# Nine weight and cache buffers as one tile, and some loads made into one load each, in a decode step with sliding-window attention and a gated unit

## The chip, the cores and the metric

The kernel runs on one core of one Trainium2 chip. A core has TensorE (PE, matrix products; PEld is its loading of the stationary operand), VectorE (DVE), ScalarE (ACT), GpSimd (POOL) and SyncE (SP), and 16 DMA engines that move data between the chip's memory (HBM) and the on-chip memory (SBUF). Matrix products land in a second on-chip memory, PSUM. The metric is the device time of one execution in microseconds (us); before the change its median is 199.18 us over three runs, which lie between 199.14 and 199.29.

## The reference

One token for each of B = 8 sequences, D = 512 wide. `s` is attention with 32 query heads over 8 shared key/value heads, on the last W = 2048 of 8192 cached positions; `g` is a gated unit 1792 wide. All inputs are bfloat16.

```python
xn = layernorm(x)
q = (xn @ wq).reshape(B, 1, 32, 128)             # wq 512 x 4096
k, v = k_cache[:, :, -W:], v_cache[:, :, -W:]    # 8 heads of 128, each for 4 query heads
s = (softmax(q k^T * 128**-0.5) v).reshape(B, 1, 4096) @ wo   # wo 4096 x 512
g = (sigmoid(xn @ w_gate) * (xn @ w_up)) @ w_down             # 512 x 1792, 512 x 1792, 1792 x 512
out = x + s * silu(g)
```

Keys and values of the window are 32 MB (2^20 bytes) each, wq and wo 4 MB each, the three other weights 1.75 MB each: some 81 million bytes are read, each once.

## The kernel before

**What is loaded.** SBUF holds nine buffers, `slot0` to `slot8`, of up to 16 KB on each of 128 partitions. Every large load takes one buffer: a tile of keys or values (half of a sequence's heads, 2 MB, `want_cache`, line 156), the gate and the up weights (`want_rows`, line 96, each in two loads of two rows per partition), the first 1408 rows of the down weights (`want_down`), and the remaining 384 rows of the down weights in eight small loads into one buffer called `side` (`want_side`, 5, 9, 5, 9, 3, 9, 3 and 9 partitions). The query weights take two buffers (rows 0 and 1, rows 2 and 3), with three side loads behind each. The output weights take four buffers: 16, 10, 4 and 2 of the 32 rows that each partition holds.

**What orders the loads.** The list `todo` holds all of them in the order of lines 171 to 192: gate, up, down, two side loads, first half of the query weights, three side loads, second half, three side loads; then key tiles with the value tiles three places behind; then the output weights. `pump` takes from the list's head as long as a buffer is empty, and `free` gives a buffer back and pumps again. So each load stands in SP's instruction queue in that order, and waits there for the last reader of the buffer's earlier content. Each load also signals its landing on one of eight completion semaphores, which all loads take in turn, those that ACT issues too: a load waits until the load eight places before it has landed. The input `x` is loaded by ACT (line 195).

**What is computed, in order of PE's queue.** Layer norm of x (DVE, ACT), its transpose, the gate product (line 278), the up product (line 294), 26 small transposes (line 328), the query product (line 352: four rows of wq, eight matmuls each; the first 16 matmuls need the first load of wq, the last 16 the second), the down product (line 366), the transposes that spread the queries, and the unit's last steps. Then the attention: for each sequence 16 half units, in each of which `k_transposes` makes eight transposes of a key tile (line 456) that DVE copies (line 461), and every second of which brings `scores` (line 474). `row_max` (line 487 and the exponentials of line 494), `p_transposes` (line 563) and `values` (line 584) follow one to three sequences behind. Lines 672 to 701 finish the last three sequences; the final tile of values is used in lines 697 and 698, and the last `turn` (line 701) writes the last column of `oP_sb`.

**The end.** The output product (lines 703 to 714) needs all of `oP_sb`. For each of the 32 rows `t` of wo it makes four matmuls (128x32 by 128x128), side by side in four column groups of the array:

```python
for t in range(RT):
    for j in range(NB):
        nc.tensor.matmul(fin_ps[Z * j : Z * (j + 1), :], lhsT=oP_sb[:, t, :],
                         rhs=weights[("wo_sb", t)][:, j * P : (j + 1) * P], ...)
```

Its first matmul waits for the load of rows 0 to 15, and those of rows 16, 26 and 30 for the three others. After it come two DVE instructions (lines 717 and 719) and four small stores.

Of the kernel before, what the change touches and what calls it, by code (L numbers as in the profile page):

```python
# [10 lines left out]
def kernel(  # L11
# [14 lines left out]
    P = 128  # L26
    B, _, D = A_x.shape
    _, Hkv, Sk, Dh = A_k_cache.shape
# [4 lines left out]
    KT = D // P  # L33
# [5 lines left out]
    CT = W // PG  # L39
# [8 lines left out]
    bf16 = mybir.dt.bfloat16  # L48
# [8 lines left out]
    slots = ctx.enter_context(tc.tile_pool(name="slots", bufs=1))  # L57
# [21 lines left out]
    q0, q1 = nc.sync, nc.scalar  # L79
    k_tiles = {}  # L80
    v_tiles = {}
    weights = {}
    rows_of = {}
    todo = []
    empty = list(range(9))

    def pump():
        while todo and (empty or not todo[0][0]):
            slot, f = todo.pop(0)
            f(f"slot{empty.pop(0)}") if slot else f()  # L90

    def free(t):
        empty.append(int(t[1][4:]))
        pump()

    def want_rows(name, w, per, r0, r1, step=None):
        def f(tag):
            t = slots.tile([P, r1 - r0, w.shape[1]], bf16, name=name, tag=tag)
            for a in range(r0, r1, step or r1 - r0):
                z = a + (step or r1 - r0)  # L100
                q0.dma_start(
                    out=t[:, a - r0 : z - r0, :],
                    in_=w.rearrange("(p r) n -> p r n", r=per)[:, a:z, :],
                )
            rows_of[(name, r0)] = (t, tag)
            for r in range(r0, r1):
                weights[(name, r)] = t[:, r - r0, :]

        todo.append((True, f))

    LOW, SF = (5, 5, 3, 3), 15
    MID, SM = 9, 4
# [3 lines left out]
    MT = 11  # L116
# [3 lines left out]
    side = {}  # L120

    def want_side(w, q, at, count, rows, base, of):
        def f(tag=None):
            if tag:
                t = slots.tile([P, SF, w.shape[1]], bf16, name="side", tag=tag)
                nc.gpsimd.memzero(t[:M_AT])  # L126
                side["t"] = t
                rows_of[("side", 0)] = (t, tag)
                for r in range(SF):
                    weights[("wd_sb", MT + r)] = t[: M_AT + MP if r < SM else SP, r]  # L130
            q0.dma_start(  # L131
                out=side["t"][at + q : at + q + 4 * (count - 1) + 1 : 4, :rows].rearrange(
                    "p s n -> p (s n)"
                ),
                in_=w[base : base + of * count * rows, :].rearrange(
                    "(p q s) n -> q p (s n)", q=of, s=rows
                )[q % of],
            )

        todo.append((not side, f))  # L140
        side["asked"] = True

    def want_down(w):
        def f(tag):
            t = slots.tile([P, MT, w.shape[1]], bf16, name="wd_sb", tag=tag)
            q0.dma_start(
                out=t[:].rearrange("p t n -> p (t n)"),
                in_=w[: MT * P, :].rearrange("(p t) n -> p (t n)", t=MT),
            )
            rows_of[("wd_sb", 0)] = (t, tag)  # L150
            for r in range(MT):
                weights[("wd_sb", r)] = t[:, r, :]

        todo.append((True, f))

    def want_cache(tiles, cache, name, b, i):
        def f(tag):
            t = slots.tile([P, CT, Dh], bf16, name=name, tag=tag)
            q0.dma_start(
                out=t[:].rearrange("p c d -> p (c d)"),  # L160
                in_=cache[b, G * i : G * (i + 1), win0:Sk, :].rearrange(
                    "l (p c) d -> p l (c d)", c=CT
                ),
            )
            tiles[(b, i)] = (t, tag)

        todo.append((True, f))

    RT = 32
    Z = 32  # L170
    want_rows("wg_sb", B_w_gate, KT, 0, KT, 2)
    want_rows("wu_sb", B_w_up, KT, 0, KT, 2)
    want_down(B_w_down)
    sides = []
    for q in range(4):
        sides.append((q, 0, LOW[q], SF, m0 + q // 2 * 2 * LOW[0] * SF, 2))
        sides.append((q, M_AT, MID, SM, m1, 4))
    for x in sides[:2]:
        want_side(B_w_down, *x)
    for i in range(2):  # L180
        want_rows("wq_sb", A_wq, KT, 2 * i, 2 * i + 2)
        for x in sides[2 + 3 * i : 5 + 3 * i]:
            want_side(B_w_down, *x)
    order = [(b, i) for b in range(B) for i in range(NQ)]
    AHEAD = 3
    for n in range(len(order) + AHEAD):
        if n < len(order):
            want_cache(k_tiles, A_k_cache, "k_sb", *order[n])
        if n >= AHEAD:
            want_cache(v_tiles, A_v_cache, "v_sb", *order[n - AHEAD])  # L190
    for t0, t1 in ((0, 16), (16, 26), (26, 30), (30, RT)):
        want_rows("wo_sb", A_wo, RT, t0, t1)

    x_bf = work.tile([B, D], bf16, name="x_bf")
    q1.dma_start(out=x_bf[:], in_=A_x.flatten_outer_dims())

    eps_t = work.tile([B, 1], f32, name="eps_t")
    nc.gpsimd.memset(eps_t[:], 1e-5)
# [8 lines left out]
        out=perm[:].rearrange("k (l p) -> k l p", l=G),  # L207
        in_=ident[:].rearrange("k (p l) -> k l p", l=G),
# [11 lines left out]
        out=rstd[:], in_=mv[:, 1:2], func=AF.Sqrt, bias=eps_t[:], scale=1.0  # L220
# [4 lines left out]
        out=xn_bf[:],  # L225
# [8 lines left out]
    for kt in range(KT):  # L234
        nc.tensor.transpose(  # L235
            out=xnT_ps[:, kt, :],
            in_=xn_bf[:].rearrange("b (p kt) -> b kt p", kt=KT)[:, kt, :],
# [53 lines left out]
    for k in range(F // FC):  # L291
        u_ps = ps_t.tile([B, FC], f32, name="u_ps", tag="t")
        for kt in range(KT):
# [8 lines left out]
            out=h_bf[:B, k * FC : (k + 1) * FC],  # L302
# [6 lines left out]
    for h in range(2):  # L309
        c = LOW[2 * h]  # L310
# [37 lines left out]
    for kt in range(KT):  # L348
        for e in range(2):
            for g in range(G):  # L350
                c0 = (G * e + g) * D
                nc.tensor.matmul(  # L352
                    q_ps[e][Z * g : Z * (g + 1), :],
                    lhsT=xnT_sb[:, kt, :],
                    rhs=weights[("wq_sb", kt)][:, c0 : c0 + D],
                    start=(kt == 0),
                    stop=(kt == KT - 1),
                    tile_position=(0, Z * g),
                    skip_group_check=True,
                )  # L360
        if kt % 2 == 1:
            free(rows_of[("wq_sb", kt - 1)])
    d_ps = ps_s.tile([P, D], f32, name="d_ps", tag="s")
    for t, k in enumerate(rows):
        g = t % G
# [206 lines left out]
    WIDE = 5  # L572

    def value(b, i, c):
        v = v_tiles[(b, i)][0][:]
        if b < WIDE:
            rows = [slice(NX * i, NX * (i + 1))]
            parts = [v.rearrange("p (j c) d -> p c j d", j=NJ)[:, c]]
        else:
            rows = [slice(Z * k, Z * (k + 1)) for k in range(NM * i, NM * (i + 1))]  # L580
            v = v.rearrange("p (m e c) d -> p m c e d", e=2, c=CU)
            parts = [v[:, m, c] for m in range(NM)]
        for r, x in zip(rows, parts):
            nc.tensor.matmul(  # L584
                o_ps[r] if b < WIDE else o_ps[r, 0:2],
                lhsT=pT[b][:, c, r],
                rhs=x,
                start=(c == 0),
                stop=(c == CU - 1),
                tile_position=(0, r.start),  # L590
                skip_group_check=True,
            )
        if c == CU - 1:
            free(v_tiles.pop((b, i)))
# [160 lines left out]
```

## Time and profile before

| | us |
|---|---|
| device time, median of three runs | 199.18 |
| device time of the profiled execution | 199.33 |
| its span, from the first to the last instruction | 197.5 |
| PE, DVE and ACT busy | 157.4, 125.4, 40.7 |
| share of the 16 DMA engines' span that the packets of SP's queue took | 96.6% |
| first matmul of the output product | 188.81 |
| first DVE instruction after the output product (line 717) | 194.19 |

The profile is one execution. Times count from the span's start. A line of its timeline reads: start, length, engine, line of the kernel, operation, out<-in, number of instructions in the group, and in brackets how long the engine was idle before it and what ended that. In the table of windows, the columns behind a stretch are its length, each engine's busy time with the number of instructions, the share of full clock that PE was granted (PEclk), the mean busy share of the 16 DMA engines, and what they moved.

### The profile page before, as it was taken

How to read it: one execution, taken by the hardware profiler on the slowest of the kernel's cores; microseconds unless marked ns; L12 is line 12 of the kernel's file. 1: busy time of each engine (PE TensorE's matmuls, PEld its weight loads, DVE VectorE, ACT ScalarE, POOL GpSimd, SP SyncE). 2: the span in 40 equal slices, each digit the busy share in tenths (PEclk: the TensorE clock that was granted, in tenths of full speed). 3: DMA queues.
4: the chain of work that ended last, by engine and by line, in shares of the span. 5: the costliest groups of instructions: out<-in, count | busy, mean ns of one | idle time of the engine just before them, and what ended most of it. 6: DMA issues, size and time to landing. Idle time of an engine off the chain costs nothing.

```text
span 197.5 us, 4796 instructions
## 1 busy us (share of the span) xinstructions
PE 157.4 (80%) x2112; PEld 103.1 (52%) x2112; DVE 125.4 (63%) x245; ACT 40.7 (21%) x95; POOL 11.0 (6%) x22
## 2 busy tenths in 40 slices
PE   0089559999788898799979987999799979976733
PEld 0034325776664565466545654566466556655531
DVE  4623106999797696679666965796669658935201
ACT  0522022006306001600160016001600160071000
POOL 8910200000000000000000000000000000000000
PEclk9999859999999999999999999999999999999975
DMA  6999999999999999999999999999999999999980
GB/s 205 424 440 435 431 434 435 425 425 431 423 425 425 438 428 435 431 425 428 422 433 431 435 425 433 428 418 428 428 438 431 428 428 431 428 423 425 428 366 21
DMA packets 6396, 81.32 MB, mean 412 GB/s; under 512 B 812, under 2 KB 820, under 8 KB 1624
## 3 DMA queue, kind: packets, MB, share of 16 engines
q1 hardware_dynamic: 6328, 81.01, 96.6%
q8 instruction: 16, 0.26, 0.5%
q10 hardware_dynamic: 48, 0.01, 0.0%
q14 instruction: 4, 0.03, 0.0%
HBM read 81.01 MB, written 0.01 MB: 410 GB/s over the span
## 4 chain that ended last, share of the span: by engine, by line
DMA 73%; PE 22%; POOL 3%; SPq 0%; issue 0%; DVE 0%; POOLq 0%
DMA v_sb<-in_A_v_cache_dram 46%; DMA wo_sb<-in_A_wo_dram 14%; PE kT_ps L456 11%; DMA wq_sb<-in_A_wq_dram 7%; DMA k_sb<-in_A_k_cache_dram 6%; PE o_ps L584 4%; PE s_ps L474 3%; POOL side L126 2%; PE m_ps L614 1%; PE fin_ps L706 1%; PE pT_ps L563 1%; SPq L131 0%; POOL perm L206 0%; POOL hT_sb L245 0%; DVE prod L717 0%
## 5 line engine op out<-in xcount | busy, mean ns | idle before, releaser
L461 DVE COPY kT_sb<-kT_ps 128x1024 bf16<-128x1024 bf16 x128 | 84.2, 683 | 28.9 <-PE kT_ps L456 25.0
L456 PE MATMUL kT_ps<-perm,k_sb 128*128 128x128 bf16 x1024 | 72.6, 220 | 3.7 <-DMA k_sb<-in_A_k_cache_dram 3.7
L456 PEld LDWEIGHTS <-k_sb 128*128 128x128 bf16 x1024 | 58.8, 98 | 26.1 <-issue 16.8
L584 PE MATMUL o_ps<-v_sb,pT_sb 128*32 128x256 bf16 (+1 forms) x352 | 36.5, 327 | 9.0 <-DMA v_sb<-in_A_v_cache_dram 7.6
L474 PE MATMUL s_ps<-kT_sb,qm_sb 128*32 128x512 bf16 x256 | 25.6, 389 | 1.3 <-DVE kT_sb L461 1.1
L494 ACT ACTIVATE p_buf<-s_ps,st 32x512 bf16<-32x512 f32 x32 | 21.7, 679 | 15.4 <-DVE st L487 15.1
L584 PEld LDWEIGHTS <-pT_sb 128*32 128x32 bf16 (+1 forms) x352 | 12.3, 101 | 21.7 <-issue 19.7
L604 ACT ACTIVATE o_sb<-o_ps,fac 128x512 f32<-128x512 f32 (+1 forms) x8 | 4.9, 608 | 60.9 <-PE o_ps L584 60.9
L568 DVE COPY pT_sb<-pT_ps 128x1024 bf16<-128x1024 bf16 x16 | 10.8, 676 | 1.8 <-PE pT_ps L563 1.8
L474 PEld LDWEIGHTS <-qm_sb 128*32 128x32 bf16 x256 | 7.0, 93 | 8.0 <-issue 1.3
L563 PE MATMUL pT_ps<-turn_rows,p_buf 128*128 128x128 bf16 x128 | 10.7, 227 | 0.0
L563 PEld LDWEIGHTS <-p_buf 128*128 128x128 bf16 x128 | 9.4, 149 | 0.2 <-issue 0.2
L521 ACT ACTIVATE w_row<-w 1x128 f32<-1x128 f32 x8 | 2.5, 309 | 30.6 <-DVE w L514 30.6
L235 PE MATMUL xnT_ps<-ident,xn_bf 8*128 8x8 bf16 x4 | 0.3, 176 | 10.6 <-DVE xn_bf L224 10.6
L385 DVE COPY qm_sb<-qT_ps 128x128 bf16<-128x128 bf16 x2 | 1.4, 881 | 8.7 <-PE qT_ps L380 8.7
L301 DVE TENSOR_TENSOR h_bf<-sig,u_ps 8x448 bf16<-8x448 f32 x4 | 2.4, 608 | 6.6 <-PE u_ps L294 6.1
L278 PE MATMUL g_ps<-wg_sb,xnT_sb 128*8 128x448 bf16 x16 | 5.7, 544 | 0.3 <-DVE xnT_sb L242 0.3
L494 ACT ACTIVATION_READ_ACCUMULATOR p_buf<-s_ps,st 32x1 f32 x32 | 5.9, 184 | 0.0
L706 PE MATMUL fin_ps<-wo_sb,oP_sb 128*32 128x128 bf16 x128 | 3.3, 263 | 3.1 <-DMA wo_sb<-in_A_wo_dram 3.1
L487 DVE TENSOR_REDUCE st<-s_ps 128x1 f32<-128x512 f32 x8 | 5.4, 681 | 0.5 <-PE s_ps L474 0.5
L235 PEld LDWEIGHTS <-xn_bf 8*128 8x128 bf16 x4 | 0.2, 117 | 10.6 <-DVE xn_bf L224 10.6
L352 PE MATMUL q_ps<-wq_sb,xnT_sb 128*32 128x512 bf16 x32 | 3.1, 526 | 3.2 <-DMA wq_sb<-in_A_wq_dram 3.2
(88 smaller groups left out, 92.0 us busy)
## 6 DMA issues: line engine op xcount, KB each, us to landing
k_sb<-in_A_k_cache_dram SPq DMA_DIRECT2D x16, 2048.0 KB
v_sb<-in_A_v_cache_dram SPq DMA_DIRECT2D x16, 2048.0 KB
wq_sb<-in_A_wq_dram SPq DMA_DIRECT2D x2, 2048.0 KB
wo_sb<-in_A_wo_dram SPq DMA_DIRECT2D x1, 2048.0 KB
wg_sb<-in_B_w_gate_dram SPq DMA_DIRECT2D x2, 896.0 KB
wu_sb<-in_B_w_up_dram SPq DMA_DIRECT2D x2, 896.0 KB
wd_sb<-in_B_w_down_dram SPq DMA_DIRECT2D x1, 1408.0 KB
wo_sb<-in_A_wo_dram SPq DMA_DIRECT2D x1, 1280.0 KB
```

The costliest lines, as they stand in the source:

```text
L126: nc.gpsimd.memzero(t[:M_AT])
L278: nc.tensor.matmul(g_ps[:], lhsT=xnT_sb[:, kt, :B], rhs=weights[("wg_sb", kt)][:, k * FC : (k + 1) * FC], start=(kt == 0), stop=(kt == KT ...
L456: nc.tensor.transpose(out=kT_ps[:, c, :], in_=k_sb[:, j * CU + h * CH + c, :], identity=perm[:],)
L461: nc.vector.tensor_copy(out=kT[(b, u)][:, h * CH : (h + 1) * CH, :], in_=kT_ps[:])
L474: nc.tensor.matmul(s_ps[b][NR * l : NR * (l + 1), :], lhsT=qm_sb[:, b, i * G + l, o : o + Z], rhs=t[:, :, PG * l : PG * (l + 1)], start=(u ...
L487: nc.vector.tensor_reduce(out=st[b][:], in_=s_ps[b][:], axis=AX.X, op=ALU.max, negate=True)
L494: nc.scalar.activation(out=p_buf[b % 2][rows, :, l, :], in_=s[rows, :].rearrange("k (c p) -> k p c", p=PG), func=AF.Exp, bias=st[b][rows, ...
L563: nc.tensor.transpose(out=pT_ps[:, c, :], in_=p_buf[b % 2][:, :, :, h * CH + c].rearrange("k p l -> k (p l)"), identity=turn_rows[:],)
L568: nc.vector.tensor_copy(out=pT[b][:, h * CH : (h + 1) * CH, :], in_=pT_ps[:])
L584: nc.tensor.matmul(o_ps[r] if b < WIDE else o_ps[r, 0:2], lhsT=pT[b][:, c, r], rhs=x, start=(c == 0), stop=(c == CU - 1), tile_position=(0 ...
L604: nc.scalar.activation(out=o[:, :n], in_=o_ps[:, :n], func=AF.Copy, scale=fac.pop(b)[:])
L706: nc.tensor.matmul(fin_ps[Z * j : Z * (j + 1), :], lhsT=oP_sb[:, t, :], rhs=weights[("wo_sb", t)][:, j * P : (j + 1) * P], start=(t == 0), ...
```

## The change

The nine buffers become one tile `ring` of [128, 9, 8192] bfloat16, and each load names a place in it (`room`). `pump` can now look for n neighbouring empty places, and holds the whole list until there are that many. `want_rows` takes a list of steps, one load each, and makes rows that lie behind each other in a partition one contiguous run.

- The up weights are one load of four rows per partition (14336 bytes on each of 128 partitions), not two of 7168. The gate weights stay two loads.
- The query weights are one load of 32768 bytes per partition over two neighbouring places, not two of 16384, and stand behind four side loads with the other four behind them.
- The output weights take two neighbouring places. Rows 0 to 25 are one load of 26624 bytes per partition, not loads of 16384 and 10240; rows 26 to 29 and 30 to 31 stay loads of their own, into the same two places.
- Both buffers of the query weights are given back together after the whole query product.
- x is loaded by four loads of two rows each. With two loads fewer for up and query weights and three more for x, the turn of the eight semaphores moves by one for the key and value tiles.

In the built program the matmuls and the other engines' instructions stand in the same order. The last half of the up product, the last half of the query product and rows 16 to 25 of the output product have no wait of their own any more: the first matmul of each product waits for the whole load. SP holds the load of the 26 rows for the last transposes of the last key tile; before, the loads of 16 and of 10 rows waited for earlier readers, and the load of 4 rows for those transposes.

```diff
-    empty = list(range(9))
+    NS = 9
+    ring = slots.tile([P, NS, CT * Dh], bf16, name="ring")
+    empty = list(range(NS))
     def pump():
-        while todo and (empty or not todo[0][0]):
-            slot, f = todo.pop(0)
-            f(f"slot{empty.pop(0)}") if slot else f()
+        while todo:
+            n, f = todo[0]
+            k = 0
+            if n:
+                found = [k for k in empty if all(k + m in empty for m in range(n))]
+                if not found:
+                    return
+                k = found[0]
+                for m in range(n):
+                    empty.remove(k + m)
+            todo.pop(0)
+            f(k)
...
+    def room(k, n, *shape):
+        size = 1
+        for x in shape:
+            size *= x
+        x = ring[:, k : k + n].rearrange("p s e -> p (s e)")[:, :size]
+        if len(shape) == 2:
+            x = x.rearrange("p (r n) -> p r n", r=shape[0])
+        return x, list(range(k, k + n))
+
+    def want_rows(name, w, per, r0, r1, steps):
+        n = -(-(r1 - r0) * w.shape[1] // (CT * Dh))
...
+            for step in steps:
                 q0.dma_start(
-                    out=t[:, a - r0 : z - r0, :],
-                    in_=w.rearrange("(p r) n -> p r n", r=per)[:, a:z, :],
+                    out=t[:, a - r0 : a - r0 + step, :].rearrange("p r n -> p (r n)"),
+                    in_=w.rearrange("(p r) n -> p r n", r=per)[
+                        :, a : a + step, :
+                    ].rearrange("p r n -> p (r n)"),
                 )
...
-    want_rows("wg_sb", B_w_gate, KT, 0, KT, 2)
-    want_rows("wu_sb", B_w_up, KT, 0, KT, 2)
+    want_rows("wg_sb", B_w_gate, KT, 0, KT, (2, 2))
+    want_rows("wu_sb", B_w_up, KT, 0, KT, (KT,))
...
-    for x in sides[:2]:
+    for x in sides[:4]:
         want_side(B_w_down, *x)
-    for i in range(2):
-        want_rows("wq_sb", A_wq, KT, 2 * i, 2 * i + 2)
-        for x in sides[2 + 3 * i : 5 + 3 * i]:
-            want_side(B_w_down, *x)
+    want_rows("wq_sb", A_wq, KT, 0, KT, (KT,))
+    for x in sides[4:]:
+        want_side(B_w_down, *x)
...
-    for t0, t1 in ((0, 16), (16, 26), (26, 30), (30, RT)):
-        want_rows("wo_sb", A_wo, RT, t0, t1)
+    want_rows("wo_sb", A_wo, RT, 0, RT, (26, 4, 2))
...
-    q1.dma_start(out=x_bf[:], in_=A_x.flatten_outer_dims())
+    for r in range(0, B, 2):
+        q1.dma_start(out=x_bf[r : r + 2], in_=A_x.flatten_outer_dims()[r : r + 2])
...
-        if kt % 2 == 1:
-            free(rows_of[("wq_sb", kt - 1)])
+    free(rows_of[("wq_sb", 0)])
```

## The prediction

> **What bounds the kernel now.** I read the page's head and slices first, then the table of windows, then the timeline around the two places that the change touches, and SP's own timeline last.
>
> ```profile
> span 197.5 us, 4796 instructions
> PEclk9999859999999999999999999999999999999975
> DMA  6999999999999999999999999999999999999980
> q1 hardware_dynamic: 6328, 81.01, 96.6%
> ```
>
> The DMA engines are busy from the first slice to the last but two. The windows say how full:
>
> ```profile
> 5.00:10.00 5.00, 0.00 (x0) 0.00 (x0) 3.19 (x5) 2.86 (x3) 5.00 (x8) 1.00 1.02 430
> 10.00:15.00 5.00, 4.17 (x15) 1.61 (x16) 1.22 (x5) 1.07 (x2) 0.44 (x2) 1.00 1.03 439
> 140.00:180.00 40.00, 35.16 (x530) 24.45 (x529) 27.60 (x57) 11.13 (x29) 0.00 (x0) 1.00 1.01 430
> 189.00:190.00 1.00, 0.89 (x64) 0.74 (x53) 0.00 (x0) 0.00 (x0) 0.00 (x0) 1.00 1.00 420
> 190.00:191.80 1.80, 0.00 (x0) 0.00 (x0) 0.00 (x0) 0.00 (x0) 0.00 (x0) 0.57 0.79 325
> 191.80:192.40 0.60, 0.54 (x24) 0.54 (x27) 0.00 (x0) 0.00 (x0) 0.00 (x0) 0.50 0.79 304
> 193.70:194.20 0.50, 0.42 (x11) 0.13 (x7) 0.01 (x1) 0.00 (x0) 0.00 (x0) 0.50 0.00 0
> ```
>
> The last column but one is the DMA share, the one before it PE's granted clock. From 5 us to 190 us the share is 1.0 at some 430 GB/s, whether the loads are of 0.9 MB (first row) or of 2 MB (third row): the stream never stops, and only a time after the stream, or a hole in it, can move the end. After 190 us the engines run out one by one, and PE's clock has fallen to half. The timeline there:
>
> ```profile
> 187.73 0.30 DVE L639 CAST oP_sb<-l_ps 128x32 bf16<-128x32 f32 x1 [0.28 <-PE l_ps L632]
> 188.81 1.08 PE L706 MATMUL fin_ps<-wo_sb,oP_sb 128*32 128x128 bf16 x64 [1.12 <-DMA wo_sb<-in_A_wo_dram]
> 191.86 2.28 PE L706 MATMUL fin_ps<-wo_sb,oP_sb 128*32 128x128 bf16 x64 [1.97 <-DMA wo_sb<-in_A_wo_dram]
> 191.86 1.06 PEld L706 LDWEIGHTS <-oP_sb 128*32 128x32 bf16 x40 [2.12 <-issue]
> 193.10 0.42 PEld L706 LDWEIGHTS <-oP_sb 128*32 128x32 bf16 x16 [0.18 <-issue]
> 193.74 0.13 PEld L706 LDWEIGHTS <-oP_sb 128*32 128x32 bf16 x7 [0.21 <-issue]
> 194.19 0.29 DVE L717 TENSOR_TENSOR prod<-gg_sb,fin_ps 128x128 f32<-128x128 f32 x1 [6.16 <-PE fin_ps L706]
> ```
>
> The output product is four bursts, one for each load of wo: 16 rows at 188.81, 10 at 191.86, 4 at 193.10, 2 at 193.74. The landings recorded for the four are 188.77, 191.82, 193.06 and 193.69, so each burst starts 0.04 us behind its load and ends before the next one lands. The time is: last landing, plus two rows, plus the finish. 64 matmuls (16 rows) took 1.08 us at full clock, 40 weight loads (10 rows) 1.06 us at half clock; read one by one, a row follows the last after 0.056 us in the first burst and after 0.107 us in the second.
>
> **The output rows, the step that sets the time.** The first 26 rows now have one landing. Loads are taken in order and the bytes ahead of row 26 are the same, so it falls where the load of 10 rows landed, 191.82, less what fewer packets save. The 16 rows that ran at 188.81 under the cover of that load have lost it: they start at 191.86 too. Before, PE waited in this stretch 0.19 us for rows 26 to 29 and 0.22 us for rows 30 and 31; those will long have landed, so 32 rows run in one piece. At half clock, with the first step 0.06 as in the burst of 191.86, the last row starts at 191.86 + 0.06 + 30 x 0.107 = 195.13, and DVE follows 0.39 us behind the last row's start, as before (193.80 to 194.19): 195.52, which is 1.33 us later. At full clock, 0.056 per row, PE would be done with row 25 by 193.3 and meet the landings of the last two loads: a cost of nothing, or a gain of about 0.1 from a faster last burst. So the ends are -0.1 and +1.33, and they are far apart.
>
> I take half clock. The nearest row is the burst at 191.86: it is the same code at the same time, and it ran at 0.50 after an idle of 1.97 us. The clock records show the fall at 190.27, 0.4 us after a burst of 1.08 us, with some 1.5 us of matmuls in the 3.4 us before. In the changed kernel that burst is gone and PE has nothing from 187.69 (the last matmul of `turn`) to 191.86, 4.2 us. The rise is slow too: PE began its gate product at 11.12, and the record has the clock rising at 16.19; it began the second half of the query product at 26.71 and the clock rose at 29.84, 3.1 us later. A run of 3.4 us that starts cold is over about when the clock would rise.
>
> [...]
>
> **Fewer packets.** The trace's packet records have one duration per size: 159 ns for 4096 bytes, 385 for 10240, 611 for 16384, which is 0.0368 ns per byte and 8.3 ns per packet. Each engine carries 8 partitions of a load, so one load less saves 8 packets, 0.066 us per engine; for up, query and output rows together 0.20 us. Against that, x in two-row loads puts its eight packets of 1024 bytes (44 ns) on fewer engines: up to three more on one, 0.13 us. The saving on the slowest engine is 0.07 to 0.20; a packet's size may also change nothing, since the windows above run at 430 and 439 GB/s with 7168 and 11264 bytes. Ends 0 and 0.20; I take 0.10, their middle.
>
> **The query weights, nothing, with cover.** Its rows:
>
> ```profile
> 22.28 1.23 PE L352 MATMUL q_ps<-wq_sb,xnT_sb 128*32 128x512 bf16 x16
> 26.71 1.90 PE L352 MATMUL q_ps<-wq_sb,xnT_sb 128*32 128x512 bf16 x16 [3.20 <-DMA wq_sb<-in_A_wq_dram]
> 32.49 1.96 PE L456 MATMUL kT_ps<-perm,k_sb 128*128 128x128 bf16 x32 [0.26 <-DMA k_sb<-in_A_k_cache_dram]
> ```
>
> The single load lands at about 26.1 to 26.7 (the second half landed at 26.67; one side load less stands ahead). All 32 matmuls then follow, at the 1.90 of the cold half twice, 3.8 us, to 29.9 to 30.5 instead of 28.6. The down product, the query transposes and DVE's copies of them shift by 1.3 to 1.9 us, and the first key tile is transposed at about 34 instead of 32.49; its landing, 32.45, stays. What hides it: PE later idles 7.6 us for value tiles and 3.7 us for key tiles, and DMA has a deep queue. Giving buffers back later delays SP by as much. The fourth key load waits for wq's landing and goes out at about 26.7; by packet durations an engine without side rows would run dry without it at 38 us, and the same reckoning gives every later load 15 us or more. If the cover were gone, it would cost up to 1.9.
>
> **SP and the two neighbouring buffers.** SP's timeline:
>
> ```profile
> 153.65 3.64 SPq L159 DMA_DIRECT2D v_sb<-in_A_v_cache_dram  x2
> 157.38 16.79 SPq L101 DMA_DIRECT2D wo_sb<-in_A_wo_dram  x4
> ```
>
> The four loads of wo were issued at 157.38, 163.50, 171.89 and 173.84. The load of 26 rows now waits for what the third waited for, so it goes out at 171.9 instead of 157.4; nothing but the other two wo loads stands behind it. The last value tile, ahead of it, landed at 183.1 to 183.9: 11 us of cover, 10 if PE is 1.3 late. Cost nothing; it would cost one for one beyond that.
>
> **The start.** The four side loads ahead of wq hold SP until the POOL clearing of `side` (done at 5.07) and then 0.69 to 0.86 us each: wq goes out at about 8.4 instead of 6.8 and 12.0, while gate, up and down keep the engines busy to 13.9. Key loads then follow at 17 instead of 20.5. x needs four issues on ACT of 0.60 us, so the last lands up to 1.8 us later than 2.7. DVE's first copy of x ran from 2.74 to 5.35, beside POOL's clearing (1.78 to 5.07), and may end at the same 5.35, at worst 2.3 later; the query product waits for wq 3.2 us longer than for this chain. Up weights by one load: the gate product ends at 16.6, long after they land at 12.0. All nothing.
>
> **Sum.** +1.33 - 0.10 = +1.23 on the profiled execution's 199.33, 200.56. The median lies 0.15 below that execution, so 200.4.
>
> **Rivals.** First, fewer loads are worth more than their packets (the other side). If each load cost the stream what its issue costs SP (0.33 to 0.63 us), three less would give back 1.0 to 1.9, at best 199.18 + 1.23 - 1.9 = 198.5; it decides from 0.5 us a load. Against it: the share is 1.02 where 0.9 MB loads follow each other. 8 in 100.
>
> [...]
>
> Second, the clock stays up or returns in the run (its fall needs not come, or a rise falls into the first microsecond): -0.1 to +0.4, about 199.1. The burst of 188.81 at full clock speaks for it, the 4.2 us without work against. 7 in 100.
>
> Third, a delay gets through: the query product's 1.3 to 1.9 us if PE never makes it up, or a hole before the 26 rows. 200.4 + 1.5 = 201.9, against 11 us of idle for DMA on PE and 11 us of cover. 8 in 100.
>
> My forecast has the remaining 77 in 100, its own range 200.0 to 200.7: the saving between 0 and 0.20 and a rise of the clock before the end. The range is 199.1 to 200.9, which takes in the second rival and leaves out the first and most of the third. About 0.2%, 0.4 us, is what a measurement of this kernel can tell from no change. Faster: 0.08 and a little of the second, 0.09. Same: the rest of the second, 0.07. Slower 0.84.
>
> **What would show it.** Right: one wait of L706 for wo at about 191.7, no burst before it, 128 matmuls in 3.4 to 3.7 us at clock 0.5, L717 near 195.4, DMA share 1.0 to 190. The first key transposes near 34 and value waits as before. Wrong: a first burst of L706 before 190, a clock of 1.0 behind 191.9, last landings before 193.0, or a window below 0.95 between 5 and 185 us.

## The result, and the profile after

The changed kernel takes 201.12 us (median of four runs, 201.06 to 201.45), against 199.24 us for the kernel before beside it (199.14 to 199.33): a ratio of 1.0098, 95% interval 1.0080 to 1.0115, or 1.88 us slower. The forecast was 200.4 us with a range to 200.9, so the sign was right and the time lies above the range. The profiled execution took 201.16 us with a span of 199.29 us, against 199.33 and 197.45 before: 1.84 us to explain.

In the new code the output product is line 731 (706 before), the two DVE instructions behind it 742 and 744 (717 and 719), the stores 746 (721), and the closing waits of the program 775 (750).

The page of the changed kernel:

```profile
span 199.3 us, 4798 instructions
PEclk9999979999999999999978999999999999999968
DMA  6999999999999999999999999999999999999940
q1 hardware_dynamic: 5896, 81.01, 95.6%
```

The same bytes move in 432 packets fewer, and the stream is full to the same place. The difference is at the end. Its timeline:

```profile
187.56 0.30 DVE L664 CAST oP_sb<-l_ps 128x32 bf16<-128x32 f32 x1 [0.28 <-PE l_ps L657]
191.62 3.26 PE L731 MATMUL fin_ps<-ring,oP_sb 128*32 128x128 bf16 x128 [4.09 <-DMA ring<-in_A_wo_dram]
194.93 0.29 DVE L742 TENSOR_TENSOR prod<-gg_sb,fin_ps 128x128 f32<-128x128 f32 x1 [7.07 <-PE fin_ps L731]
195.25 0.29 DVE L744 TENSOR_TENSOR y_bf<-prod,x_f 128x128 bf16<-128x128 f32 x1
195.57 1.09 SPq L746 DMA_DIRECT2D out_dram<-y_bf  x2
195.57 0.65 ACTq L746 DMA_DIRECT2D out_dram<-y_bf  x2
```

Before, SP's line read:

```profile
194.82 0.67 SPq L721 DMA_DIRECT2D out_dram<-y_bf  x2
```

**First, the output product.** The four bursts have become one, behind one landing, and `y_bf` is ready at 195.54 instead of 194.80: 0.74 us later. The windows, with PE's clock in the last column but two, show why it was not more:

```profile
188.00:191.60 3.60, 0.00 (x0) 0.01 (x1) 0.00 (x0) 0.00 (x0) 0.00 (x0) 0.91 0.84 352
191.60:194.20 2.60, 2.58 (x100) 2.58 (x103) 0.00 (x0) 0.00 (x0) 0.00 (x0) 0.50 0.30 114
194.20:195.00 0.80, 0.68 (x40) 0.50 (x30) 0.07 (x1) 0.00 (x0) 0.00 (x0) 0.89 0.00 0
```

PE ran at 0.50 of its clock for 2.8 us, and the clock record then rises at 194.38: the rows follow each other after 0.107 us up to there and after 0.056 us behind it.

**Second, SP's two stores.** The line of SP says 1.09 us for two instructions, where it was 0.67. They take 0.33 and 0.31 us, as before within 0.02, but the second begins 0.46 us after the first ends (195.90 to 196.36), where the gap was 0.06. That is 0.41 us.

**Third, the landing of that second store.** SP's closing waits, in the view of waits, first after and then before:

```profile
SPq L775 <- DMA out_dram<-y_bf: 1.4, 2, 1.2
```

```profile
SPq L750 <- DMA out_dram<-y_bf: 0.7, 3, 0.4
```

The longest single wait is 1.2 us instead of 0.4. Before, the second store landed 1.41 us after its issue began (195.21 to 196.62), now 2.10 us (196.36 to 198.46): 0.69 us. Seven of the eight signals of the store had come by 197.64; the eighth came at 198.46. The DMA records show what was beside it. This is the view of transfers between 196.9 and 197.5:

```profile
DMA packets 15, 0.01 MB, mean 17 GB/s; under 512 B 14, under 2 KB 14, under 8 KB 14
q14 instruction: 1, 0.01, 3.2%
q1 hardware_dynamic: 14, 0.00, 2.4%
```

A packet of 8192 bytes on queue 14, which the profile calls `instruction`, runs from 197.30 to 197.60, and the last packet of the store (256 bytes) starts at 197.60, 0.41 us behind the packet before it. Its signal followed 0.86 us after that, where the others came some 0.45 us after their packets; why, the trace does not show. In the kernel before, the packet of that kind that came last is found in the window from 174 to 178, at 176.0, in the middle of the load stream:

```profile
q1 hardware_dynamic: 114, 1.72, 100.8%
q14 instruction: 1, 0.01, 0.5%
```

Within the span both kernels have four such packets; the first three stand at 50, 103 and 123 us in each. Only the fourth has moved, from 176.0 to 197.3.

0.74 + 0.41 + 0.69 = 1.84 us, the whole difference of the spans.

### The profile page after: what moved, and what is told of

It is laid out like the page before. It is cut to its first block, busy times and chain, and to the rows that moved or that the text cites. A ratio compares the mean times of both kernels' runs of the same rounds, so it can differ in the third digit from the quotient of the medians.

```text
span 199.3 us, 4798 instructions
## 1 busy us (share of the span) xinstructions
PE 158.9 (80%) x2112; PEld 104.8 (53%) x2112; DVE 124.2 (62%) x245; ACT 40.7 (20%) x95; POOL 10.8 (5%) x22
## 4 chain that ended last, share of the span: by engine, by line
DMA 78%; PE 13%; DVE 2%; POOL 2%; SPq 1%; issue 1%; POOLq 0%
DMA ring<-in_A_k_cache_dram 46%; DMA ring<-in_A_v_cache_dram 13%; DMA ring<-in_A_wo_dram 10%; DMA ring<-in_A_wq_dram 9%; PE kT_ps L481 5%; PE o_ps L609 2%; PE fin_ps L731 2%; POOL ring L153 2%; PE q_ps L378 1%; SPq L158 1%; PE s_ps L499 1%; DVE kT_sb L486 1%; PE d_ps L391 1%; PE m_ps L639 1%; PE pT_ps L588 1%
## 5 line engine op out<-in xcount | busy, mean ns | idle before, releaser
L481 PE MATMUL kT_ps<-perm,ring 128*128 128x128 bf16 x1024 | 73.3, 221 | 2.5 <-DMA ring<-in_A_k_cache_dram 2.5
L481 PEld LDWEIGHTS <-ring 128*128 128x128 bf16 x1024 | 59.5, 99 | 25.1 <-issue 18.3
L609 PE MATMUL o_ps<-ring,pT_sb 128*32 128x256 bf16 (+1 forms) x352 | 37.0, 330 | 8.2 <-DMA ring<-in_A_v_cache_dram 6.7
L239 DVE CAST x_f<-x_bf 8x512 f32<-8x512 bf16 x1 | 3.3, 3298 | 7.0 <-DMA x_bf<-in_A_x_dram 7.0
L731 PE MATMUL fin_ps<-ring,oP_sb 128*32 128x128 bf16 x128 | 3.3, 293 | 4.1 <-DMA ring<-in_A_wo_dram 4.1
L304 PE MATMUL g_ps<-ring,xnT_sb 128*8 128x448 bf16 x16 | 6.1, 578 | 0.3 <-DVE xnT_sb L268 0.3
L731 PEld LDWEIGHTS <-oP_sb 128*32 128x32 bf16 x128 | 3.2, 137 | 4.1 <-issue 3.6
```

The costliest lines, as they stand in the source:

```text
L304: nc.tensor.matmul(g_ps[:], lhsT=xnT_sb[:, kt, :B], rhs=weights[("wg_sb", kt)][:, k * FC : (k + 1) * FC], start=(kt == 0), stop=(kt == KT ...
L481: nc.tensor.transpose(out=kT_ps[:, c, :], in_=k_sb[:, j * CU + h * CH + c, :], identity=perm[:],)
L609: nc.tensor.matmul(o_ps[r] if b < WIDE else o_ps[r, 0:2], lhsT=pT[b][:, c, r], rhs=x, start=(c == 0), stop=(c == CU - 1), tile_position=(0 ...
```

## The experiments

The theory from the two traces has two halves. A: the 26 rows behind one landing run with PE's clock at half. B: the fourth instruction packet belongs to SP, which asks for it after a fixed count of its own instructions; no view names the engine that a packet is for. The changed kernel has three SP loads less (50 loads and stores on SP instead of 53), so the point is not right behind the last load of the output weights any more but between SP's two stores. Counted in the two traces, the 80th instruction of SP is the last load of the output weights before and the second store now. The main rival is that the merged early loads, the one tile or the new order cost time themselves. All runs stand beside the kernel before on the same chip.

**Output weights alone split again** (`wo_split`):

```diff
-    want_rows("wo_sb", A_wo, RT, 0, RT, (26, 4, 2))
+    want_rows("wo_sb", A_wo, RT, 0, RT, (16, 10, 4, 2))
```

> The changed kernel, but with the output rows in loads of 16, 10, 4 and 2 again (into the same two neighbouring places); all else as changed. SP issues 51 loads and stores instead of 50. Two parts of the 1.88 us are to be told apart: A, the output product starts 0.74 us later at its end (L742 at 194.93 against 194.19) because 26 rows wait for one landing; B, the time from the last DVE instruction to the end grew by 1.1 us, where the trace shows SP's second store 0.46 us late and a packet of 8192 bytes on queue 14 (instruction fetch) at 197.3 on the engine that carries the store's last 256 bytes. Theory: A goes and B stays, since SP still has two wait-only instructions and stores at the same places of its stream: bursts of 16, 10, 4 and 2 rows, first one before 190, L742 near 194.0, fetch still behind 195, device time 200.0 to 200.3. Rival (B hangs on the late product itself, by its place in time): both go, 199.0 to 199.2. Rival (A is not from the one landing): 201.0.

Measured 200.21 us (200.11 to 200.57, four runs) against 199.12: ratio 1.0059, interval 1.0042 to 1.0076. The end of its timeline:

```profile
191.79 2.25 PE L731 MATMUL fin_ps<-ring,oP_sb 128*32 128x128 bf16 x64 [0.97 <-DMA ring<-in_A_wo_dram]
194.08 0.29 DVE L742 TENSOR_TENSOR prod<-gg_sb,fin_ps 128x128 f32<-128x128 f32 x1 [4.93 <-PE fin_ps L731]
194.72 1.10 SPq L746 DMA_DIRECT2D out_dram<-y_bf  x2
```

A is gone: DVE starts at 194.08, 0.11 us sooner than before. B is all there: the gap between the stores (0.46 us), the instruction packet at 196.17 to 196.59, and the second store landing 1.81 us after its issue (before 1.41). The span of 198.33 is 0.88 above that of before: -0.11 for the product, +0.42 for the gap, +0.40 for the landing, and 0.17 for something new, the closing waits, on which the fifth experiment bears.

**Up and query weights split again, the 26 rows kept** (`up_wq_two`):

```diff
-    want_rows("wu_sb", B_w_up, KT, 0, KT, (KT,))
+    want_rows("wu_sb", B_w_up, KT, 0, KT, (2, 2))
-    want_rows("wq_sb", A_wq, KT, 0, KT, (KT,))
+    want_rows("wq_sb", A_wq, KT, 0, KT, (2, 2))
```

> The changed kernel, but with the up weights in two loads of two rows and the query weights in two loads of two rows; the output rows stay one load of 26, then 4 and 2. SP has two more loads ahead of the stores. Theory (SP's fetch comes after a fixed number of its instructions; before, it fell behind the last load of the output rows, at 176.0, and with fewer loads it falls into the stores): the fetch of 8192 bytes on queue 14 comes at 173 to 177 again, the stores follow each other without the gap of 0.46 us, B of 1.1 us is gone and A stays: device time 199.9 to 200.2, L742 near 194.9. Rival (the late end comes from the x loads on ACT or from the turn of the semaphores): B stays, 201.0 to 201.3. Rival (the larger loads cost or save by themselves): the landing of row 25, 191.58 in the changed kernel, moves by more than 0.3 us.

Measured 200.57 us (200.22 to 200.69, four runs) against 199.12: 1.0068, 1.0053 to 1.0083. With two SP loads more, the instruction packet stands at 177.3, the stores are 0.06 us apart (195.57, 195.95), and the last one lands at 197.37. So B's two parts went. The time is more than expected. The profiled execution is the fastest of the four; the others took 200.45 to 200.69 and have no trace. In the profiled one SP still took four closing waits behind that landing, to 197.63. The 58 loads and stores of this kernel take the eight semaphores in turn, and SP's closing waits go through the semaphores in a fixed order, so that here the last store is not on the semaphore that is waited for last.

**All three split again, one tile and x in four loads kept** (`all_split`): the two edits above together.

> The changed kernel, but with the up, query and output weights in the same loads as before (2+2, 2+2, 16+10+4+2 rows); one tile with places, the other order of the side loads, and x in four loads stay. Theory: both parts go, 199.0 to 199.3, so the one tile and the order cost nothing. Rival (the places, x in four loads, or the turn of the semaphores cost something): over 199.6.

Measured 199.54 us (199.43 to 199.61, ten runs) against 199.12: 1.0019, 1.0010 to 1.0029. Nearly all of the 1.88 us is back, but not all: again the last store's wait comes early (at 196.63), and five more waits follow to 196.94, where the kernel before ended its closing waits at 196.64.

**x in one load** (`x_one`), else the changed kernel:

```diff
-    for r in range(0, B, 2):
-        q1.dma_start(out=x_bf[r : r + 2], in_=A_x.flatten_outer_dims()[r : r + 2])
+    q1.dma_start(out=x_bf[:], in_=A_x.flatten_outer_dims())
```

> The changed kernel, but with x in one load on ACT, as before. ACT has three instructions less, SP the same number of loads. x lands near 2.7 again, not 7.0. Theory: nothing of it reaches the end; the fetch of SP stays behind 195 and costs as much or, if it slips past the stores' packets, less; 200.0 to 201.3 with L742 at 194.7 to 195.5. Rival (the x loads delay the fetch of ACT or lengthen the early chain): the fetch goes back to 176 or earlier and the time falls to 199.9 to 200.1, or the part A shrinks.

Measured 200.62 us (200.41 to 200.92, four runs) against 199.12: 1.0074, 1.0059 to 1.0089.

```profile
192.02 3.61 PE L730 MATMUL fin_ps<-ring,oP_sb 128*32 128x128 bf16 x128 [4.15 <-DMA ring<-in_A_wo_dram]
195.67 0.29 DVE L741 TENSOR_TENSOR prod<-gg_sb,fin_ps 128x128 f32<-128x128 f32 x1 [7.47 <-PE fin_ps L730]
196.32 0.67 SPq L745 DMA_DIRECT2D out_dram<-y_bf  x2
```

Here A is whole: no rise of the clock before 196.28, and DVE starts 3.65 us after the product, as the prediction reckoned (0.06 + 30 x 0.107 + 0.39 = 3.66). The stores have no gap, since SP has a small instruction less ahead of them; the instruction packet comes at 198.07, behind the stores. It stays at the end although ACT again issues only the three loads and stores that it had before, so ACT's count is not what places it. The product ends 1.48 us later than before and the closing waits 1.69 us later.

**All split, and x in one load** (`all_split_x1`): the edits of `all_split` and `x_one` together, which makes 56 loads and stores again, as the kernel before has.

> The run with up, query and output weights in the loads of before, but x in one load again, so that the number of loads, 56, and with it the stores' four semaphores are those of before. Theory (SP's closing waits go through the eight semaphores in one order, 0.06 us each; before, the stores hold the last four, while with three loads more the last store holds the third and five waits follow its landing): the 0.31 us between the last landing and the last wait go, device time 199.0 to 199.25. Rival (the one tile or the order of the side loads costs the 0.42 us): 199.5 again.

Measured 199.18 us (198.84 to 199.39, ten runs) against 199.19: 0.9998, 0.9989 to 1.0008. So one tile, `room`, the new `pump` and the order of the side loads cost nothing that this measurement can tell. It also shows what the order of the closing waits does; first this kernel, then `all_split`:

```profile
SPq L774 <- DMA out_dram<-y_bf: 0.9, 4, 0.4
```

```profile
SPq L775 <- DMA out_dram<-y_bf: 1.1, 1, 1.1
```

With 56, each of the four stores has a wait of its own, in the order in which they land, and nothing follows the last. In `all_split`, with 59, there is one wait of 1.1 us, on the store that lands last, and the others are gone through behind it; `up_wq_two`, with 58, has one such wait too. The two kernels differ by 0.36 us in the median (each beside its own runs of the kernel before, 199.18 against 199.19 and 199.54 against 199.12), some of which may be x. The four loads of x in the changed kernel make 56 too (53 on SP and 3 on ACT before, 50 and 6 after), so this cost is not in its 1.88 us.

**Three SP loads less in the kernel before** (`before_act3`): both loads of the up weights and the load of the down weights are issued by ACT. No load is merged, and SP has 50 loads and stores as in the changed kernel.

```diff
             t = slots.tile([P, MT, w.shape[1]], bf16, name="wd_sb", tag=tag)
-            q0.dma_start(
+            q1.dma_start(
...
-                q0.dma_start(
+                (q1 if name == "wu_sb" else q0).dma_start(
                     out=t[:, a - r0 : z - r0, :],
```

> The kernel before, with three of SP's loads (both of the up weights, and the first 1408 rows of the down weights) issued by ACT instead; no place, load size or landing of the output rows is changed, and the number of loads stays, so each store keeps its semaphore. SP's stream is then as long up to its stores as in the changed kernel (50 loads and stores, 28 wait-only instructions ahead of the end). Theory (SP's instruction fetch falls into the stores and costs by itself): bursts of 16, 10, 4 and 2 rows and L717 near 194.2 as before, but the fetch of 8192 bytes at 195.5 to 197.5, SP's second store 0.4 us late, and the last landing 0.4 to 1.2 us later: device time 199.6 to 200.3. Rival (the late stores belong to the changed loads): 199.0 to 199.3 with the fetch near 176.

Measured 202.29 us (201.85 to 202.84, four runs) against 199.19: 1.0158, 1.0134 to 1.0182. That is 2 us more than expected, and two things have to be kept apart. With three loads moved to ACT the early stream got a hole:

```profile
20.00:25.00 5.00, 2.74 (x36) 1.32 (x35) 0.20 (x1) 0.30 (x2) 0.74 (x3) 0.57 0.90 385
25.00:30.00 5.00, 3.24 (x31) 1.20 (x30) 0.00 (x0) 1.08 (x2) 0.00 (x0) 0.50 0.93 365
```

The share of the DMA engines is 0.90 and 0.93, so `prod` starts at 195.82, 1.63 us later. I had not foreseen that. What was asked is answered by the end of the timeline:

```profile
195.82 0.29 DVE L717 TENSOR_TENSOR prod<-gg_sb,fin_ps 128x128 f32<-128x128 f32 x1 [4.89 <-PE fin_ps L706]
196.46 1.09 SPq L721 DMA_DIRECT2D out_dram<-y_bf  x2
```

and among the waits of SP

```profile
SPq L750 <- DMA out_dram<-y_bf: 1.4, 2, 1.2
```

The 1.09 us of SP and the wait of 1.2 us are those of the changed kernel to the digit. The packet of queue 14 stands at 198.15 to 198.47, and from the end of `y_bf` to the last landing it is 2.88 us instead of 1.82. B costs 1.06 us here with no merged load, no `ring` and the output product in four bursts as before.

**The 26 rows alone, without B and with 56 loads and stores** (`up_wq_two_x2`): `up_wq_two` with x in two loads of four rows.

```diff
-    for r in range(0, B, 2):
-        q1.dma_start(out=x_bf[r : r + 2], in_=A_x.flatten_outer_dims()[r : r + 2])
+    for r in range(0, B, 4):
+        q1.dma_start(out=x_bf[r : r + 4], in_=A_x.flatten_outer_dims()[r : r + 4])
```

> The changed kernel with up and query weights in two loads each and x in two loads, which makes 56 loads and stores again. Only the single landing of the 26 rows is left of what reached the end: fetch early, stores on the last four semaphores. Theory: the end of the output product is late by 0.7 to 1.5 us by where the clock's windows fall, nothing else: 199.9 to 200.5, and 0.1 to 0.2 us less than with x in four loads. Rival (the turn of the semaphores is worth nothing): 200.6 as there.

Measured 200.30 us (200.24 to 200.56, four runs) against 199.19: 1.0059, 1.0043 to 1.0076.

```profile
191.60 3.61 PE L731 MATMUL fin_ps<-ring,oP_sb 128*32 128x128 bf16 x128 [3.25 <-DMA ring<-in_A_wo_dram]
195.26 0.29 DVE L742 TENSOR_TENSOR prod<-gg_sb,fin_ps 128x128 f32<-128x128 f32 x1 [6.56 <-PE fin_ps L731]
195.90 0.68 SPq L746 DMA_DIRECT2D out_dram<-y_bf  x2
```

A alone costs 1.11 us in the median and 1.10 us in the span (198.56 against 197.45). The product takes 3.66 us from its start to DVE's again.

**The same with PE kept busy** (`up_wq_two_x2_warm`): 16 more matmuls, whose results nothing reads, between the last `turn` and the output product.

```diff
     turn(last, l_ps[:, P : P + RT])
+    warm_ps = ps_t.tile([P, 512], f32, name="warm_ps", tag="t")
+    for _ in range(16):
+        nc.tensor.matmul(
+            warm_ps[:], lhsT=ident[:], rhs=p_buf[0][:].rearrange("p a g c -> p (a g c)")[:, :512],
+            start=True, stop=True,
+        )
```

> The run before it with 16 extra matmuls (128x128 by 128x512, into an unread PSUM tile) between the last turn and the output product, some 3.4 us of work for PE from 187.9 to 191.4. They change no result. Theory (the single landing costs through PE's clock, which falls in the gap of 4 us): the clock stays 1.0, rows follow each other after 0.056 us instead of 0.107, PE ends behind the landings of rows 30 and 31, L742 at 193.9 to 194.2: 198.9 to 199.2. Rival (the cost is the number of rows behind one landing, at any clock): 199.9 or more. If the extra work runs past the landing at 191.7, the gain is smaller by as much.

Measured 199.09 us (198.93 to 200.66, ten runs) against 199.19: 1.0010, 0.9989 to 1.0032. Seven of the ten runs lie between 198.93 and 199.18; three took 199.66, 200.56 and 200.66 and have no trace; the two longest are as slow as the kernel without the extra matmuls, and whether the clock fell in them is not known. The profiled one:

```profile
188.45 3.61 PE L729 MATMUL warm_ps<-p_buf,ident 128*128 128x512 bf16 x15
192.00 1.97 PE L737 MATMUL fin_ps<-ring,oP_sb 128*32 128x128 bf16 x128
194.02 0.29 DVE L748 TENSOR_TENSOR prod<-gg_sb,fin_ps 128x128 f32<-128x128 f32 x1 [5.08 <-PE fin_ps L737]
```

and its window:

```profile
191.90:194.00 2.10, 2.07 (x129) 1.80 (x128) 0.00 (x0) 0.00 (x0) 0.00 (x0) 1.00 0.29 105
```

The same single landing, the same 128 matmuls, clock 1.0, and DVE starts at 194.02 instead of 195.26. So in this execution, and by their times in most of the ten, the single landing costs nothing but PE's clock. A is shown with the clock down and with it up.

**Towards a better version** (`merged_wo4`): the changed kernel with the output weights in four loads, and the gate weights as one load too, which keeps 56 loads and stores.

```diff
-    want_rows("wg_sb", B_w_gate, KT, 0, KT, (2, 2))
+    want_rows("wg_sb", B_w_gate, KT, 0, KT, (KT,))
-    want_rows("wo_sb", A_wo, RT, 0, RT, (26, 4, 2))
+    want_rows("wo_sb", A_wo, RT, 0, RT, (16, 10, 4, 2))
```

> The changed kernel with the output weights in four loads again (16, 10, 4 and 2 rows), and with the gate weights too as one load: gate, up and query weights are one load each, x stays in four. The number of loads is that of the changed kernel, so the four stores keep the last four semaphores; SP has two small instructions less, so its instruction fetch should come behind its second store, where the kernel with x in one load had it without harm. My theory (single landing, fetch and semaphores are all that the change costs, and every load saved is 0.07 us): the output product is four bursts again, first DVE instruction behind it at 194.0 to 194.15, stores without a gap, 198.9 to 199.1 us, a ratio of 0.9985 to 0.9995. The rival that merging the early loads costs something of its own: 199.4 to 200.0. If the fetch falls between the stores: 200.2, as with the output weights alone split.

Measured 199.32 us (199.14 to 199.56, eleven runs) against 199.16: 1.0008, 0.9999 to 1.0016. The end behaves as expected: four bursts, SP's stores 0.05 us apart, the instruction packet at 196.69, behind them. SP has 50 loads and stores as in the changed kernel, but two small instructions less ahead of the stores; its 80th instruction is now the second closing wait, and SP stands still for 0.46 us in front of that one (195.62 to 196.07), while the stores are still on their way. But the three merged loads brought nothing, since the last landings are not sooner (bursts at 191.96, 193.17 and 193.79, before 191.86, 193.10 and 193.74). The windows say where the saving went:

```profile
20.00:25.00 5.00, 3.77 (x39) 2.19 (x37) 2.45 (x5) 0.00 (x0) 1.23 (x4) 0.99 0.95 411
25.00:30.00 5.00, 3.74 (x36) 1.60 (x39) 0.19 (x1) 0.75 (x3) 0.00 (x0) 0.50 0.96 412
```

In these two windows the kernel before moved 428 and 434 GB/s. 39 GB/s less over 5 us are 0.195 MB, 0.45 us at 430 GB/s. All five kernels with the query weights as one load have such a dip at 20 to 25 us (411 to 418 GB/s: the changed kernel, `x_one`, `wo_split`, this one and the next), and the six with two loads of them and with all weights on SP have none (428 to 441). What holds the stream there was not taken apart.

**And with PE kept busy** (`merged_wo4_warm`): the same with the 16 matmuls.

> The same, with 16 more matmuls (128x128 by 128x512, into a PSUM tile that nothing reads) between the last turn and the output product. By my theory they keep PE's clock at 1.0 until the last two rows, which then take 0.06 us less each and end their matmuls sooner: 0.1 to 0.25 us below the kernel without them, 198.7 to 198.95. If the clock falls all the same before 193.5, the same time as without them.

Measured 199.37 us (198.99 to 200.76, twelve runs) against 199.16: 1.0023, 1.0005 to 1.0040.

```profile
189.07 3.61 PE L729 MATMUL warm_ps<-p_buf,ident 128*128 128x512 bf16 x15
192.61 1.97 PE L737 MATMUL fin_ps<-ring,oP_sb 128*32 128x128 bf16 x128
194.63 0.29 DVE L748 TENSOR_TENSOR prod<-gg_sb,fin_ps 128x128 f32<-128x128 f32 x1 [5.08 <-PE fin_ps L737]
```

The clock stayed up (1.00 in the windows from 188 to 196), but the extra matmuls stand in PE's queue ahead of the product. In this execution the last `turn` came 0.62 us later than in the other kernel with them, and the product, whose first 26 rows had landed by 192.01, began behind them at 192.61. Here the fixed number of matmuls cost more than the clock gave, and the gain of 0.1 to 0.25 us that was expected did not come in the median either. No version was found that beats the kernel before by more than the measurement can tell.

## Why the prediction was right and wrong

**What set the time: right.** One wait of the output product at 191.62 (forecast 191.7), no burst before it, half clock at its start, and the two later loads landed under it. That the cold clock is the whole cost of the single landing was the forecast's reason, and `up_wq_two_x2` and its warm counterpart show it: 1.11 us with the clock down, nothing with it up in the profiled execution. `up_wq_two_x2`, which has the 26 rows but no fetch among its stores, took 200.30 us, where 200.4 had been forecast for the whole change.

**The output rows, +1.33: right as a price, too high for the profiled execution.** A whole cold run takes 3.65 and 3.66 us in the two kernels where the clock did not rise in it, as reckoned. In the profiled execution of the changed kernel the clock rose at 194.38, so the run took 3.31 us from start to DVE. With the product's start 0.24 sooner, the step came to +0.74. The prediction had allowed for such a rise in its own range of 200.0 to 200.7, and said it would be about when the run is over. The trace cannot tell how the other three runs went.

The clock records show how it varied. In the traces of the kernel before and of the changed one every change of the record lies a whole multiple of 3.41 us from the others of its trace. Where the clock came back, the record of the lowered clock lasts one such piece (190.97 to 194.38 in the changed kernel, 190.81 to 194.22 in `up_wq_two`) or two (188.81 to 195.64 in `up_wq_two_x2`, 189.46 to 196.28 in `x_one`), although the product starts at nearly the same time in all four (191.60 to 192.02). In the changed kernel PE worked 2.76 us in the piece that ended at 194.38, and the clock rose; in `up_wq_two_x2` only 0.62 us in the piece that ended at 192.23, and it rose one piece later. Ahead of the fall, PE had nothing in a whole piece in the changed kernel (187.56 to 190.97). In `up_wq_two_x2` the clock fell after a piece in which PE had worked 1.96 us, and in the kernel before, at 190.27, after one with 1.53 us of matmuls, so the low clock did not need a whole piece without work. What sets where a piece begins is not shown.

**The step that failed: "SP and the two neighbouring buffers ... Cost nothing", and with it a sum that ends at `y_bf`.** The step looked at when SP issues each load and who stands behind it, and found 11 us of cover, rightly: the 26 rows went out at 171.68 and cost nothing by that. It did not ask what three SP loads fewer do to the packet taken for SP's instruction fetch, which went from 176.0 to 197.3. The sum took everything behind `y_bf` as unchanged; it measured +0.41 and +0.69, 1.10 us of the 1.84. The third rival (a delay gets through, 201.9) had the direction of the miss but not its mechanism: no delay reached the output product, and what came late lies behind it.

**Fewer packets, -0.10: the sign held in this execution, the account did not.** The 26 rows landed at 191.57 instead of 191.82, 0.25 sooner (the forecast's ends were 0 and 0.20). But the windows show two parts that the account did not have: up to 20 us the stream was ahead by 0.47 us (342 against 316 GB/s from 2 to 5 us, 437 against 430 to 10 us, 443 and 446 against 439 and 432 in the next two windows of 5 us, together 0.203 MB at 430 GB/s), and between 20 and 30 us it lost 0.29 us of that (415 and 422 against 428 and 434). In `merged_wo4`, where the gate weights are merged too, the burst of rows 16 to 25 started 0.10 us later than before. A load saved there is not 0.066 us won.

**The first rival (fewer loads are worth more, 198.5): wrong.** `merged_wo4` has the gate, up and query weights in three loads less and is not faster than before (1.0008, 0.9999 to 1.0016).

**The query weights: nothing, right, with the wrong numbers.** The forecast had 32 cold matmuls in 3.8 us and the first key transposes at about 34. They took 2.68 us from 26.13, and the key transposes began at 32.55 (before 32.49). The reason is the start, which was off too: the four loads of x, issued among the weights' loads (0.73 to 2.16), landed at 7.0 us and not by 4.5, the gate product began at 14.28 instead of 11.12, 3.2 us later and beyond the worst case named, and PE was still at full clock when the query weights came (the record falls at 27.13). All of it was hidden, and `all_split`, which keeps the late x, bounds what it can have cost: 0.42 us with the closing waits in it.

**The range.** Its upper end, 200.9, left out the third rival for its chance of 8 in 100, and the time came out 0.2 us above it. The end behind `y_bf` had no term at all, so it had no bounds either.

## What to carry to other kernels

When loads are merged or moved, follow the engine that issues them to its last instruction: here what is taken for its last instruction fetch went, where it was counted, with its 80th instruction, waits included, and where it fell between the closing stores it cost 0.8 to 1.1 us, while in the middle of the load stream, or behind the stores, no cost of it could be seen. Before a product that closes the kernel, a split load is worth more than its packets, if the early rows are done under cover of the later landings, as here; behind a single landing all rows run at whatever clock PE has after its wait (3.66 us and a cost of 1.10 in `up_wq_two_x2`, 2.02 us in its warm counterpart). And when the number of loads changes, look at which of the turn-taking semaphores the last stores end up on (about 0.3 us here).

## What the runs showed of the hardware

- **An instruction fetch at the end.** What is taken here for SP's fetch is one packet of 8192 bytes on the queue `instruction` (197.30 to 197.60 in the changed kernel). In the three kernels where it followed SP's first store (the changed one, `wo_split`, `before_act3`), SP stood still for 0.46 us between its two stores, the packet began 0.6 to 1.0 us behind the gap, and the second store landed 0.4 to 0.7 us later after its issue than before. In the other kernels it fell at 176 to 178 us or behind the second store, and the gap was 0.05 to 0.07 us. In the three, the second store is SP's 80th instruction in the trace; in `merged_wo4` and `merged_wo4_warm` the 80th is the second closing wait, and the same halt stands in front of it; in the kernel before it is the last load of the output weights. That the halt is the request for that packet is inferred from this coincidence; the place moved with SP's instruction count. In the three, the halt and the late landing together cost 1.10, 0.82 and 1.06 us.
- **The order of the closing waits.** SP went through the completion semaphores in the same order in the changed kernel, `wo_split`, `up_wq_two` and `all_split`, whichever the last store was on, some 0.06 us for each wait that was already over. Whether the last store is on the last of them decided about 0.3 us here (`all_split` against `all_split_x1`, with x as the only other difference).
- **Small loads behind large ones.** The loads of x, 8 KB in all, landed at 7.0 us as four loads, at 5.3 us as two (`up_wq_two_x2`) and at 2.7 us (before) or 3.0 us (`x_one`) as one, with the weights' loads issued by SP from 0.73 us on.
